# Loads of the next k, v and q held back until all four transposing DMAs of a batch have landed, with the work from the third batch on ordered anew

## The chip, the cores and the metric

The kernel runs on one core of a Trainium2 chip. Its time is the device time of one execution in microseconds (us), lower is better, and the comparison is between the kernel before and the kernel after one change. The core has four engines that compute, each with its own stream of instructions: TensorE (PE, with PEld for its weight loads), VectorE (DVE), ScalarE (ACT) and GpSimd (POOL). SyncE (SP) does nothing here but issue DMAs. An engine works its stream in order, and an instruction may wait for semaphores that other engines or landed DMAs have raised.

## The reference, cut to what matters

A linear attention over 8 batches of 8 heads, 576 rows and 64 columns a head, with an RMS norm, is followed by a residual MLP of width 512. The MLP first mixes the 576 rows (tokens) and then the columns (channels, 512 to 2048 and back).

```python
kv  = np.einsum('bhsd,bhse->bhde', k, v)
out = np.einsum('bhsd,bhde->bhse', q, kv)
rms = np.sqrt(np.mean(out * out, axis=-1, keepdims=True) + 1e-06)
x   = out / rms * g_norm          # heads side by side: (8, 576, 512)
a1  = alpha1 * x + beta1
u   = x + lam * np.einsum('ts,bsd->btd', w_tok, a1)
a2  = alpha2 * u + beta2
res = u + lam * (np.maximum(a2 @ w_ch1, 0.0) @ w_ch2)
```

## The kernel before

**Batches.** The 8 batches are numbered 0 to 7. The 576 rows of one are held as four blocks of 128 rows and a tail of 64; the tails of an even batch and of the odd one behind it share one tile of 128 rows (`xt`, transposed `a2l`). `xm` has four places for the blocks of batches, `a2m` two for their transposes.

**Stages of a batch.** `kv` (L639, L645) multiplies k by v in f32. `norm` makes a block of the attention's output: PE products from `kvc` and the transposed q (L730, f32), then square, sum, root and scaling on ACT and DVE (L697 to L715, the last step L715 writing x), and on POOL the token mixer's operand `rm` (L718). `tok` is the token mixing (PE L813) with its residual add on DVE (L823, which writes `xm`). `a2_dma` turns a finished block round so that the channel MLP can contract over channels: POOL casts it to bf16 (`a2b`, L901), then a DMA of SP's queue transposes it into `a2m` (L914). `ch1` (PE L1091) multiplies `a2m` by the first weights, ACT applies the relu into `hh` or `ht` (L920). The second product goes by a scheme of fewer, wider combinations of blocks (`strassen`, PE L1213 with 256 columns; sums of blocks on DVE, L1175; kept products are copied by ACT, L1243, and added into `xm` by POOL, L1246; the last addends come from DVE, L1251). For batches 0 and 1 it is plain (`ch2`, L1152), and for batches 6 and 7 ch1 runs for both together (`pair`). `store` sends a finished block out by SP's queue (L1343, L1348, L1265).

**What is woven.** While the MLP of batch b runs, `attention(b + 2)` and `mix(b + 2)` are written behind it, and the order below weaves them into its products, so that PE always has some product to do.

**The loads.** `attention(b)` issues the loads of batch b + 1, which go into the buffers that batch b has just been read from: k and v by POOL's queue, each as 512 rows (1 MB, L1467, `kr` and `vr`) and 64 tail rows (L1471), and q by SP's queue in four pieces with 32-column rows (L1459, `qs`). All are tied to a transposing DMA of the batch before through the list `landing`:

```python
load_kv(b + 1, landing.get(b - 1, ()))                              # L1524
load_q(b + 1, landing.get(b - 1, [P.lastw[("w2", 3)][0]]))          # L1525
```

`landing[b]` is set by `a2_dma`, which is called for c = 0 to 3 (the blocks) and, in odd batches, for c = 4 (the shared tails):

```python
if c < 3:                                                           # L916
    landing[b] = [o]                                                # L917
```

Each call overwrites the entry, so that the loads of batch b + 2 wait for the transposing DMA of block 2 of batch b, and for no other. The DMAs of block c signal one semaphore a c: d_50 to d_53 for blocks 0 to 3, d_54 for the tails; d_38 is that of v's tail rows.

**The order.** Nothing is scheduled on the chip or by a compiler. Every operation gets a number as it is written, and a table `ORDER` lists the numbers in the order in which they are put into the engines' streams (`op:bank` names the PSUM bank of a product, `a+b` weaves two groups of products). A second table, `GATES`, adds waits: `i: j` makes operation i wait for j. `Prog.replay` reads both, and `synchronize` turns what depends on another engine or on a DMA into semaphores. Numbers that matter below: 448, 452, 456 and 460 are batch 2's four casts (L901), 650 to 657 steps of `weight_sums`, which prepares weight sums on DVE; 586 to 589, 747 to 750, 940 to 943 and 1093 to 1096 are q loads, each gated on the tail rows of the same batch's k or v.

Of the kernel before, what the change touches and what calls it, by code (L numbers as in the profile page):

```python
# [103 lines left out]
"""  # L104

GATES = {23: 52, 38: 67, 39: 73, 40: 163, 124: 151, 125: 213, 204: 196, 233: 269, 234: 216, 235:
# [8 lines left out]


class Op:


    __slots__ = ("tile", "q", "kind", "cost", "lat", "fns", "idx", "deps", "raw", "alloc", "tiles", "at",  # L120
                 "pos", "waits", "inc", "clock", "slot", "nbytes", "ns", "val", "form", "bias")

    def __init__(self, q, kind, cost, lat, fns, pri, idx):
# [236 lines left out]
def bass_transnormer_attn__then__resmlp_affine_kernel(  # L360
# [15 lines left out]
    with ExitStack() as stack:  # L376
# [515 lines left out]
        def a2_dma(b, c, t=None):  # L892
# [20 lines left out]
            o = P.dma(  # L913
                "SP", "t%d" % c, 0.7, lambda e: e.dma_start_transpose(dst, a2b[:, c]),  # L914
                r=[("a2b", c)], w=dk, issue=0.6)
            if c < 3:  # L916
                landing[b] = [o]  # L917

        def relu(dst, t, keys, f=None):
            P.op("ACT", act(512, 0 if f is None else 1), lambda e: e.activation(  # L920
# [704 lines left out]
```

## Time and profile before

| | |
|---|---|
| Runs, us | 334.7, 330.46, 332.15 (median 332.15) |
| Profiled execution, us | 332.92 |
| Its span, from the first to the last instruction, us | 331.1 |
| Mean granted clock of TensorE | 0.990 |
| DMA | 48.15 MB in 108,532 packets, 145 GB/s mean |

The profile is of one execution of the kernel. Its page gives the busy time and share of each engine, the span in 40 equal slices (of 8.28 us here; a digit is the busy share in tenths, PEclk the clock that TensorE was granted), the DMA queues, the chain of work that ended last (each step followed back to what released it), and the costliest groups of instructions, as line, engine, operation and tiles with count, busy time and mean. Other views are asked for: waits by what released them, a timeline of a stretch, the busy times in a list of stretches, and of DMAs the time from issue to landing. SPq is SP's queue: its rows are the issue of DMAs, not their transfer. A wait for several semaphores shows as one for the last of them.

The costliest single groups of PE's instructions are L1091 (ch1, 96.8 us), L1213 (strassen, its largest group 43.9), L730 (norm, 43.2), L1152 (ch2, 36.8), L639 (kv, 34.7) and L813 (token mixing, 29.3).

### The profile page before, as it was taken

Reading aid. Unit: us, or ns where it says so; the run is one execution under the profiler, and the core shown is the slowest. Engines: PE = TensorE matmul, PEld = TensorE weight load, DVE = VectorE, ACT = ScalarE, POOL = GpSimd, SP = SyncE. Lnnn points to the kernel's source line nnn. Section 1 sums busy time; section 2 is a strip of 40 time slices with the busy share of each in tenths; the row PEclk is TensorE's granted clock in tenths of the full one; section 3 lists DMA queues with packets and bytes.
Section 4 is the critical chain, followed back from the end, with each engine's and each line's share of the span. In section 5 each row is a group of like instructions: output and inputs, shape, how many; then the busy total and the mean of one; then the engine's idle time right before and its main releaser. Section 6 shows DMA issues by size and latency. Waiting matters only on the chain.

```text
span 331.1 us, 6149 instructions
## 1 busy us (share of the span) xinstructions
PE 322.1 (97%) x2411; PEld 220.3 (67%) x2441; DVE 251.3 (76%) x460; ACT 176.8 (53%) x362; POOL 140.1 (42%) x146
## 2 busy tenths in 40 slices
PE   8999999999999999969999999999999999999996
PEld 8777664555766455847558975587658554579985
DVE  3595178776999998706986389898899889997673
ACT  5674772249444473614872566742785057865440
POOL 3699036998063353610625241727135600012320
PEclk9999999999999999969999999999999999999999
DMA  7999998999912991995825992796050150000125
GB/s 259 319 259 258 215 247 196 198 143 259 272 40 48 263 207 25 159 226 124 206 33 122 231 177 61 133 305 104 34 157 3 40 166 4 0 2 0 50 88 183
DMA packets 108532, 48.15 MB, mean 145 GB/s; under 512 B 82061, under 2 KB 101717, under 8 KB 108504
## 3 DMA queue, kind: packets, MB, share of 16 engines
q1 hardware_dynamic: 72160, 25.00, 33.1%
q0 software_dynamic: 26800, 21.38, 32.9%
q10 hardware_dynamic: 9544, 1.39, 2.5%
q8 instruction: 19, 0.31, 0.4%
q14 instruction: 9, 0.07, 0.1%
HBM read 38.82 MB, written 9.44 MB: 146 GB/s over the span
## 4 chain that ended last, share of the span: by engine, by line
PE 88%; DVE 4%; DMA 3%; ACT 2%; SPq 1%; POOL 1%; issue 1%
PE ps L1091 24%; PE ps L1213 22%; PE ps L1152 9%; PE ps L813 9%; PE ps L1032 7%; PE ps L730 3%; DMA a2m<-a2b 3%; PE ps L639 2%; PE ps L1105 2%; PE ps L973 2%; PE ps L466 1%; SPq L914 1%; PE ps L595 1%; PE ps L858 1%; DVE small L781 1%; PE ps L617 1%
## 5 line engine op out<-in xcount | busy, mean ns | idle before, releaser
L1091 PE MATMUL ps<-a2m,w 128*128 128x512 bf16 x369 | 96.8, 386 | 0.4 <-issue 0.2
L718 POOL TENSOR_TENSOR rm<-xm,la_bc 128x512 bf16<-128x512 f32 x28 | 35.4, 1272 | 68.4 <-DVE xm L715 50.0
L1091 PEld LDWEIGHTS ps<-a2m,w 128*128 128x128 bf16 x384 | 36.4, 98 | 40.8 <-DMA a2m<-a2b 3.4
L920 ACT ACTIVATE hh<-ps,b 128x512 bf16<-128x512 f32 x72 | 47.2, 686 | 12.4 <-PE ps L1091 7.8
L1246 POOL TENSOR_TENSOR xm<-xm,tmp 128x512 f32<-128x512 f32 x18 | 22.7, 1268 | 60.0 <-ACT sq L983 28.2
L730 PE MATMUL ps<-kvc,qt 128*128 128x128 f32 (+1 forms) x140 | 43.2, 409 | 3.3 <-DMA a2m<-a2b 3.3
L1213 PE MATMUL ps<-w,hh 128*128 128x256 bf16 x344 | 43.9, 279 | 0.0
L1213 PEld LDWEIGHTS ps<-w,hh 128*128 128x128 bf16 x344 | 34.1, 100 | 7.1 <-issue 0.7
L1152 PE MATMUL ps<-w,hh 128*128 128x512 bf16 x137 | 36.8, 385 | 0.1
L639 PE MATMUL ps<-vr,kr 128*128 128x128 f32 x112 | 34.7, 408 | 0.0
L1251 DVE TENSOR_TENSOR xm<-ps,xm 128x512 f32<-128x512 f32 x24 | 16.3, 686 | 21.9 <-PE ps L1213 14.8
L700 DVE TENSOR_REDUCE small<-sq 128x8 f32<-128x512 f32 (+1 forms) x35 | 23.3, 678 | 10.3 <-ACT sq L697 10.1
L813 PE MATMUL ps<-rm,wt 128*128 128x512 bf16 x108 | 29.3, 382 | 0.3 <-issue 0.2
L730 PEld LDWEIGHTS ps<-kvc,qt 128*128 128x128 f32 (+1 forms) x140 | 27.6, 198 | 2.1 <-ACT qt L1480 0.4
L901 POOL CAST a2b<-xm 128x512 bf16<-128x512 f32 x24 | 14.2, 611 | 32.6 <-DVE xm L823 18.5
L697 ACT ACTIVATE sq<-ps 128x512 f32<-128x512 f32 (+1 forms) x35 | 20.5, 594 | 13.2 <-PE ps L730 12.9
L708 DVE TENSOR_TENSOR ps<-ps,small 128x512 f32<-128x512 f32 (+1 forms) x35 | 24.3, 696 | 0.8
L920 ACT ACTIVATE hh<-ps 128x512 bf16<-128x512 f32 x32 | 17.5, 597 | 11.9 <-PE ps L1091 11.8
L639 PEld LDWEIGHTS ps<-vr,kr 128*128 128x128 f32 x112 | 22.4, 200 | 1.6
L1243 ACT ACTIVATE tmp<-ps 128x512 f32<-128x512 f32 (+1 forms) x20 | 11.5, 575 | 20.6 <-PE ps L1213 20.6
L1152 PEld LDWEIGHTS ps<-w,hh 128*128 128x128 bf16 x144 | 13.4, 97 | 13.4 <-issue 0.4
L1480 ACT ACTIVATE qt<-qp 128x576 fp32r<-128x576 f32 x24 | 15.9, 679 | 11.1 <-DVE qp L1477 11.0
(216 smaller groups left out, 618.2 us busy)
## 6 DMA issues: line engine op xcount, KB each, us to landing
out_dram<-xm SPq DMA_DIRECT2D x32, 256.0 KB, 2.4
kr<-in_k_dram POOLq DMA_DIRECT2D x7, 1024.0 KB, 6.7
vr<-in_v_dram POOLq DMA_DIRECT2D x7, 1024.0 KB, 8.2
qs<-in_q_dram SPq DMA_DIRECT2D x20, 288.0 KB, 5.0
w<-in_moe_w_ch_dram POOLq DMA_DIRECT2D x8, 512.0 KB, 10.5
xm<-in_q_dram SPq DMA_DIRECT2D x8, 288.0 KB, 5.1
qs<-in_v_dram SPq DMA_DIRECT2D x4, 288.0 KB, 5.4
w<-in_k_dram SPq DMA_DIRECT2D x4, 288.0 KB, 5.4
```

The source lines that it names most:

```text
L639: P.mm("fill", 128, [lambda e, t=t, c=c, h=h, o=128 * (h % 4): e.matmul(t.ap()[:, o:o + 128], kr4[:, h, c:c + 2, :].rearrange("p c d -> p ...
L700: P.op("DVE", dve(n), lambda e: e.tensor_reduce(out=st, in_=sq[rs, s3, 0:nst, :], axis=AX.X, op=ALU.add), r=[("sq", s3)], w=[("sm", s4)])
L708: P.op("DVE", dve(n), lambda e: e.tensor_tensor(out=grp(ps()), in0=grp(ps()), in1=st[..., None].to_broadcast([rs.stop - rs.start, nst, DH] ...
L718: P.op("POOL", pool(n), lambda e: e.tensor_tensor(out=r, in0=x.rearrange("p h e -> p (h e)"), in1=la, op=ALU.mult), r=xks + ["la"], w=rks)
L730: P.mm("fill", 128, [lambda e, p=p: e.matmul(dst(p), qt[:, p, cs], kvc[:, i, p, :], start=(p == 0), stop=(p == 3)) for p in range(4)], r=[ ...
L813: P.mm("fill", 512, [lambda e, sc=sc: e.matmul(t.ap(), wt[:, sc if sc < 4 else tw(b), 128 * c:128 * c + 128], rsrc(b, sc, al), start=(sc = ...
L920: P.op("ACT", act(512, 0 if f is None else 1), lambda e: e.activation(dst, t.ap(), ACT.Relu, bias=0.0 if f is None else b1[:, f:f + 1]), r ...
L1032: P.mm("main", 512, [lambda e, i=i: e.matmul(t.ap(), lhs[:, i, 128 * x + o:128 * x + o + 128], rhs[:, i, :], start=(first and i == 0), sto ...
L1091: P.mm("main", 512, [lambda e, dj=dj: e.matmul(t.ap(), w1[:, dj, 128 * fj:128 * fj + 128], a2m[:, b % 2, dj, :], start=(dj == 0), stop=(dj ...
L1152: P.mm("main", 512, [lambda e, fj=fj, t=t, c=c: e.matmul(t.ap(), (ht[:, fj, 128 * c:128 * c + 128] if c < 4 else hl[:, fj, :]), w2[:, fj, ...
L1213: P.mm("main", 256, [lambda e, c=c, fj=fj: e.matmul(t.ap()[:, 256 * c:256 * c + 256], at[:, fj, 128 * c:128 * c + 128], rhs(fj), start=(fi ...
L1246: P.op("POOL", pool(256 * n), lambda e, cs=cs, f=f: e.tensor_tensor(out=X[:, cs, f], in0=X[:, cs, f], in1=two(tmp[:, s]), op=ALU.add), r=x ...
```

## The change

`landing[b]` becomes, for batches 3 and up, the list of the transposing DMAs of all four blocks. The loads of batches 5, 6 and 7 so wait for all four of batches 3, 4 and 5. For batches up to 2 the entry stays that of block 2 alone, and the tails (c = 4) are in no list. The tables are written anew: `ORDER` from about 95 us of the program on (in the streams, from row 258 of PE's), and `GATES` in part. No operation is added or removed; each engine has as many instructions as before.

```diff
 GATES = {23: 52, 38: 67, 39: 73, 40: 163, 124: 151, 125: 213, 204: 196, 233: 269, 234: 216, 235:
-    260, 237: 298, 371: 465, 379: 650, 399: 275, 448: 654, 452: 654, 466: 465, 468: 650, 586:
-    585, 587: 585, 588: 585, 589: 585, 597: 651, 621: 651, 632: 652, 636: 652, 640: 652, 644:
+    260, 237: 298, 371: 465, 379: 650, 399: 275, 448: 654, 452: 655, 456: 655, 460: 655, 466:
+    465, 468: 467, 586: 585, 587: 585, 588: 585, 589: 585, 597: 533, 605: 656, 613: 656, 632:
...
-406:4+498:1 414:5+534:7 468 379 495 407 408 422:2+535 415 416 430:0+536 502:3 469 423 499 431 503
...
             o = P.dma(
                 "SP", "t%d" % c, 0.7, lambda e: e.dma_start_transpose(dst, a2b[:, c]),
                 r=[("a2b", c)], w=dk, issue=0.6)
-            if c < 3:
-                landing[b] = [o]
+            if c < 4:
+                landing[b] = landing.get(b, []) + [o] if b > 2 else [o] if c < 3 else landing[b]
```

What the streams look like at the places that matter is shown below: the line, the operation with its tiles (written, then read) and the shape, the semaphores that it waits for in brackets, and x for equal ones in a row.

**The loads of batch 5 on POOL.** The four loads stand behind the cast of the shared tails of batches 2 and 3. Before:

```order
L901 CAST a2b<-xt 128x512 [waits s_DVE]
L1471 DMA vr<-in_v_dram 64x8x64 [waits d_52]
L1471 DMA kr<-in_k_dram 64x8x64
L1467 DMA vr<-in_v_dram 128x8x256
L1467 DMA kr<-in_k_dram 128x8x256
L1246 TENSOR_TENSOR xm<-xm,tmp 128x2x256 [waits s_ACT,s_DVE]
L1246 TENSOR_TENSOR xm<-xm,tmp 128x2x256 [waits s_ACT] x2
```

and after:

```order
L901 CAST a2b<-xt 128x512 [waits s_DVE]
L1471 DMA vr<-in_v_dram 64x8x64 [waits d_52,d_50,d_51,d_53]
L1467 DMA vr<-in_v_dram 128x8x256
L1467 DMA kr<-in_k_dram 128x8x256
L1246 TENSOR_TENSOR xm<-xm,tmp 128x2x256 [waits s_DVE,s_ACT]
L1246 TENSOR_TENSOR xm<-xm,tmp 128x2x256 [waits s_ACT]
L1246 TENSOR_TENSOR xm<-xm,tmp 128x2x256
L1471 DMA kr<-in_k_dram 64x8x64
```

The first load waits for four transposes where it waited for one, and the load of k's tail rows moved behind the three adds.

**The adds of batch 2's token mixing on DVE**, with the last step of a norm (L715) and the sums of weights for batch 1's last products and batch 2's first (L1175, L1133) among them. Before:

```order
L823 TENSOR_TENSOR xm<-ps,xm 128x512 [waits s_PE] x3
L715 TENSOR_TENSOR xt<-ps,g_bc 64x512
L823 TENSOR_TENSOR xm<-ps,xm 128x512 [waits s_PE]
L700 TENSOR_REDUCE small<-sq 128x8 [waits s_ACT]
L1175 TENSOR_TENSOR ws<-w,ab_bc 128x1024
L1133 TENSOR_SCALAR w<-w,ab 128x2048 [waits s_PE]
L1133 TENSOR_SCALAR w<-w,ab 128x2048 [waits s_DVE]
```

and after:

```order
L823 TENSOR_TENSOR xm<-ps,xm 128x512 [waits s_PE]
L1175 TENSOR_TENSOR ab_bc<-w 128x1024
L823 TENSOR_TENSOR xm<-ps,xm 128x512 [waits s_PE]
L715 TENSOR_TENSOR xt<-ps,g_bc 64x512
L823 TENSOR_TENSOR xm<-ps,xm 128x512 [waits s_PE]
L1175 TENSOR_TENSOR ws<-w,ab_bc 128x1024 [waits s_DVE]
L823 TENSOR_TENSOR xm<-ps,xm 128x512 [waits s_PE]
L700 TENSOR_REDUCE small<-sq 128x8 [waits s_ACT]
```

The adds, which the casts L901 of batch 2 wait for, now have three other operations between them, where they had one.

**The transposes of batch 2 and the q loads of batch 4 on SP.** Before:

```order
L914 DMA_TRANSPOSE a2m<-a2b 128x4x128 [waits s_POOL] x3
L914 DMA_TRANSPOSE a2m<-a2b 128x4x128
L1343 DMA out_dram<-xm 128x512
L1459 DMA qs<-in_q_dram 32x72x32 [waits d_38]
L1459 DMA qs<-in_q_dram 32x72x32 x3
```

and after:

```order
L914 DMA_TRANSPOSE a2m<-a2b 128x4x128 [waits s_POOL]
L1343 DMA out_dram<-xm 128x512 x2
L914 DMA_TRANSPOSE a2m<-a2b 128x4x128 [waits s_POOL] x3
L1459 DMA qs<-in_q_dram 32x72x32 [waits d_38]
L1459 DMA qs<-in_q_dram 32x72x32 x3
L1348 DMA out_dram<-xt 64x512 [waits s_DVE]
```

Two stores of finished blocks now stand between the first transpose and the other three.

133 rows, old and new, of tables (GATES, ORDER) are left out of this document.

## The prediction

> **What bounds the kernel now.** The page first: busy shares, the slices, the chain that ended last.
>
> ```profile
> PE 322.1 (97%) x2411; PEld 220.3 (67%) x2441; DVE 251.3 (76%) x460; ACT 176.8 (53%) x362; POOL 140.1 (42%) x146
> PE   8999999999999999969999999999999999999996
> PEclk9999999999999999969999999999999999999999
> PE 88%; DVE 4%; DMA 3%; ACT 2%; SPq 1%; POOL 1%; issue 1%
> ```
>
> PE is busy 97% of 331.1 us, and the two rows by slices show one hole, in slice 18 (about 141 to 149 us), where PE and its granted clock both fall to 6 tenths. The waits of PE, longest first, and the stretches around that hole (us; busy time of PE, PEld, DVE, ACT, POOL; granted clock; DMA share; GB/s) come next.
>
> ```profile
> PE ps L730 <- DMA a2m<-a2b: 3.3, 1, 3.3
> PE ps L466 <- DVE fil L465: 1.0, 1, 1.0
> PE ps L813 <- issue: 0.2, 1, 0.2
> ...
> 135.00:141.40 6.40, 6.40 (x60) 5.62 (x58) 3.78 (x6) 2.94 (x5) 5.07 (x6) 1.00 1.44 190
> 141.40:144.70 3.30, 0.07 (x2) 0.02 (x2) 0.69 (x1) 0.00 (x0) 0.50 (x1) 0.83 1.71 300
> 144.70:150.50 5.80, 5.77 (x24) 3.79 (x26) 0.09 (x1) 1.18 (x2) 0.00 (x0) 0.51 0.80 141
> ```
>
> PE stood 3.3 us for a transposing DMA, and then worked 5.8 us at a clock of 0.51. No other wait of PE after the first microseconds is above 0.2 us. So whatever a new order does, it can win little beyond this hole, and it can lose anywhere. The timeline of the queues (start us, duration) tells which transfers met there.
>
> ```profile
> 130.53 3.02 SPq L914 DMA_TRANSPOSE a2m<-a2b  x2
> ...
> 133.64 0.74 POOL L1471 DMA_DIRECT2D vr<-in_v_dram  x1 [1.54 <-DMA a2m<-a2b]
> ...
> 134.23 2.61 SPq L914 DMA_TRANSPOSE a2m<-a2b  x2
> ...
> 135.03 0.93 POOL L1467 DMA_DIRECT2D vr<-in_v_dram  x1
> ...
> 135.93 0.92 POOL L1467 DMA_DIRECT2D kr<-in_k_dram  x1
> ```
>
> The queue of SP issued batch 3's block transposes 2, 0 (130.53) and 1, 3 (134.23, so the last about 135.6). POOL waited for number 2 alone and put batch 5's loads between them. Landing times (min/median/max) of single transposes: all 28 with their median, then the last one of batch 3, of batch 2 (issued 106.56) and of batch 5 (212.16).
>
> ```profile
> DMA to landing us min/median/max: 2.4/2.5/9.1
> DMA to landing us min/median/max: 9.1/9.1/9.1
> DMA to landing us min/median/max: 4.9/4.9/4.9
> DMA to landing us min/median/max: 5.7/5.7/5.7
> ```
>
> 2.5 us is the common case; the three slow ones all had the 1 MB loads in flight. 135.6 + 9.1 = 144.7 is the moment PE starts again.
>
> **The change, part by part.**
>
> 1. *Four waits instead of one, batch 3.* The loads of batch 5 now start when all four transposes have landed, so number 3 meets none of them. At 2.5 us it lands at 135.6 + 2.5 = 138.1, which is 3.3 us before PE runs dry at 141.4. Gain: the 3.3 us, whole. What hides the transpose from then on is the batch 2 products that stand ahead of ch1(3); were they shorter by 3.3 us, the wait would be back.
>
> 2. *The clock after it.* From 144.7 to 150.5 PE did 5.8 x 0.51 = 2.96 us of full-speed work; without the hole 2.84 us fall away too. Row first: the clock fell inside a hole of 3.3 us (0.83 on average, so for about a third of it). The Trainium skill, "TensorE: Matmul & The Clock Gate", section "What's actually happening", says the clock halves after at least one idle window of about 3.4 us, and that the windows run free of the kernel. By that figure alone a 3.3 us hole would cost no clock, and the sum would be 332.9 - 3.3 + 0.8 = 330.4; the measured clock decides. Gain of 1 and 2: 6.1 us.
>
> 3. *Batch 4 and its loads of batch 6.* The last transpose of batch 4 was issued at 174.95 and lands 2.5 us later, at 177.45; the first load of batch 6 starts behind that:
>
> ```profile
> 174.95 1.27 SPq L914 DMA_TRANSPOSE a2m<-a2b  x1
> ...
> 177.78 0.95 POOL L1467 DMA_DIRECT2D kr<-in_k_dram  x1
> ```
>
> So the added wait is 0 here.
>
> 4. *Batch 5 and its loads of batch 7.* The first of them was issued at 211.0, and it now starts when the last transpose lands. That one was issued at 212.16, so 212.16 + 2.5 = 214.7, or 3.7 us later. The lower end is the 1.5 us that POOL stood ahead of batch 3's loads, if the new order issues all four transposes as closely. The two 1 MB loads were issued last but one and last, at 212.4 and 213.3; landings of POOL's loads there stand between the first issue and the first product that reads them:
>
> ```profile
> 210.99 0.74 POOL L1471 DMA_DIRECT2D vr<-in_v_dram  x1
> ...
> DMA to landing us min/median/max: 7.7/9.3/10.9
> ...
> 229.37 0.30 PE L639 MATMUL ps<-vr,kr 128*128 128x128 f32 x1
> ```
>
> The later one landed at 213.3 + 10.9 = 224.2, and its first product starts at 229.37: 5.2 us of cover against 1.5 to 3.7. Cost 0. The q loads queue on SP behind them (the gates tie them to v's tail rows), 12.6 us of issue from 214.15, and are read by the DVE transposes at 232.24. They landed about 2.4 us ahead (229.9 = last issue 225.5 + 4.4). What is moved is the start; the bytes are the same, and the loads no longer share with transposes: 0 to 1.3 us, taken 0.
>
> ```profile
> 214.15 12.59 SPq L1459 DMA_DIRECT2D qs<-in_q_dram  x4
> DMA to landing us min/median/max: 4.4/9.2/12.2
> 232.24 0.77 DVE L1477 STREAM_TRANSPOSE qp<-qs 128x576 f32<-128x576 f32 x1
> ```
>
> 5. *What queues behind POOL's wait.* Now the three adds of batch 2's kept products (L1246) stand behind a wait to about 138.1 and three issues of 0.7 to 0.9 us: up to 2.5 us later than the 138.17 of this row.
>
> ```profile
> 138.17 3.72 POOL L1246 TENSOR_TENSOR xm<-xm,tmp 128x512 f32<-128x512 f32 x3 [1.33 <-DVE hh L1175]
> ```
>
> DVE's last adds (L1251) need them, and PE's next products need the banks these free. The new order puts the transpose's landing nearer to its cast, and a norm with a product and ch1(3)'s first tile (1.7 + 0.9 us of PE) between the last product and the first that needs the bank. Ends 0 and 1.3 us, taken 0.
>
> 6. *The third batch (batch 2) keeps the wait for transpose 2 alone, and its order is new.* Before and now:
>
> ```profile
> 100.73 2.00 DVE L823 TENSOR_TENSOR xm<-ps,xm 128x512 f32<-128x512 f32 x3
> 102.64 0.67 DVE L715 TENSOR_TENSOR xt<-ps,g_bc 64x512 f32<-64x512 f32 x1
> 104.62 0.71 DVE L1175 TENSOR_TENSOR ws<-w,ab_bc 128x1024 bf16<-128x1024 bf16 x1
> ...
> 102.06 1.72 POOL L901 CAST a2b<-xm 128x512 bf16<-128x512 f32 x3 [4.43 <-DVE xm L823]
> 106.71 0.95 POOL L1467 DMA_DIRECT2D kr<-in_k_dram  x1 [1.93 <-DMA a2m<-a2b]
> ...
> 102.70 5.13 SPq L914 DMA_TRANSPOSE a2m<-a2b  x4
> ...
> 108.61 2.98 PE L1152 MATMUL ps<-w,hh 128*128 128x512 bf16 x12
> 111.58 1.67 PE L1091 MATMUL ps<-a2m,w 128*128 128x512 bf16 x7
> ```
>
> Transpose 0 was issued last (106.56) and landed 4.9 us later at 111.5, when PE wanted it at 111.58: no slack at all. In the new order the cast for transpose 2 comes behind L715 and L1175 on DVE: 102.73 + 0.67 + 0.71 = 104.1, cast 0.6, issue 104.8, where it was 103.94. That is 0.86 us later. Two transposes follow it as before, so the last meets the kr load at the same distance (0.15 us) and lands at 111.5 + 0.86 = 112.35. Cost 0.8 us of PE wait; ends 0 (if the last landed in 2.5 us) and 5.0 us (if it took 9.1: 107.4 + 9.1 = 116.5 against 111.5). I take 0.8, because the geometry is that of the row with 4.9. So short a hole is below the 2.3 us that passed before the clock fell in the measured one, so no clock is lost.
>
> 7. *The rest of the order.* The counts of products are the same. Twelve of L730's products now stand among 256-column products (three norms woven with L1213). A weight load of f32 takes 0.19 to 0.20 us and a 256-column product 0.11 (x48 in 5.24), so the ends are 0 and 12 x 0.09 = 1.1 us. Where one followed such a product, the next product started 0.15 us after it, not later than in the steady pattern (0.29 a pair). I take 0.
>
> ```profile
> 172.48 5.24 PE ps L1213 x48
> 151.92 0.19 PEld L730 LDWEIGHTS ps<-kvc,qt 128*128 128x128 f32 x1
> 151.95 0.30 PE L730 MATMUL ps<-kvc,qt 128*128 128x128 f32 x1
> 152.10 0.39 PE L1091 MATMUL ps<-a2m,w 128*128 128x512 bf16 x1
> ```
>
> Sum: -3.3 - 2.8 + 0.8 = -5.3. The profiled execution took 332.92 us (span 331.1 and 1.8 around it), so 327.6. It lies 0.8 above the median of the runs, 332.15, from which the same sum gives 326.9. I say 327.4, 1.4% under the median.
>
> **The rivals.**
>
> *A. The third batch's last transpose is hit in full.* Batch 3's number 3 had v's 1 MB load 0.55 us ahead of it and took 9.1; batch 2's last had kr's 0.15 behind it and took 4.9. If two stores now ahead of transpose 2 on SP move the last one behind the load, PE waits 116.5 - 111.5 = 5.0 us and about 2.9 us go with the clock: 332.9 - 6.1 + 7.9 = 334.7, above before. It decides from a landing of about 7.5 us on, where wait and clock together pass 6.1. For it: no slack, and this batch alone got no added wait. Against: the distance between the two issues follows from one wait and does not change.
>
> *B. The waits come back elsewhere.* Points 4, 5 and 7 each at the upper end (1.3, 1.3, 1.1 us), in part: 329 to 331.
>
> *C. The loads are not what slows the transpose.* If load and transposes merely took turns, a transpose would at most double, from 2.5 to 5.0 us. The 4.9 and nearly the 5.7 fit that, and the 9.1 does not. Then part of the 9.1 comes from SP's own queue, where a store (at 133.6, between the two pairs of transposes) stands ahead, and the new order has stores there too. The wait is back in full if nothing of the 9.1 goes: 333 us, no change; a wait of any size needs more than 141.4 - 135.6 = 5.8 us. For it: that number. Against: the median of all 28 is 2.5, though stores stand on SP's queue around many of them. The Trainium skill, "DMA: Bandwidth & Descriptors", section "Queues, rings and completion order", has a DMA engine go round between the queues it has work for, a whole packet each; that is the taking of turns, told as a rule, and of the three slow landings the trace agrees on two.
>
> *D. More than 2%.* The hole and its clock are all that PE can win: 332.9 - 6.1 = 326.8 is the floor, and 2% under the median is 325.5. It needs runs of before with a longer hole than the profiled one (the slowest of three took 334.7).
>
> **How the numbers follow.** Forecast 0.62 (326.0 to 328.8), A 0.09, B 0.14, C 0.06, D 0.09. The likeliest is 327.4. The range 325.6 to 331.0 holds the forecast and B and leaves out A, C and most of D, together about 0.2. Two per cent of 332.15 is 6.6 us, about what a measurement of this kernel can tell from no change: faster by more 0.13, within 0.83, slower by more (over 338.8, A and B together) 0.04. So I expect a real gain of some 5 us that stays inside that bound.
>
> **What would show it.** Batch 3's four transposes land in 2.4 to 3 us; PE has no wait for one there; the clock reads 1.0 in the slices around 145 us. Near 112 us PE waits about 0.8 us for batch 2's last transpose, with a landing near 5. The first POOL load of batch 5 waits for the transposes, and L1246 behind it is not on the chain. I am wrong if a second hole above 2 us shows in the row of PE, if the clock falls anywhere past 60 us, or if batch 3's last transpose still takes over 5 us.

## The result, and the profile after

| | before | after |
|---|---|---|
| Median of the runs, us | 332.13 (330.31 to 334.7, 6 runs) | 327.12 (326.38 to 328.19, 6 runs) |
| Profiled execution, us | 332.92 | 327.01 |
| Its span, us | 331.1 | 325.2 |
| Mean granted clock of it | 0.990 | 1.000 |

The ratio is 0.985, with a 95% interval of 0.980 to 0.990: faster by 1.5%, a gain that is clear of noise and inside the 2% that the chances went by. The forecast was 327.4. Here and below, ratios leave out executions more than 1.5% above the fastest of the same kernel, while counts of executions by their clock take all of them.

The busy shares, the slices and the chain of the page of the changed kernel:

```profile
PE 320.0 (98%) x2441; PEld 218.7 (67%) x2441; DVE 252.1 (78%) x460; ACT 176.7 (54%) x362; POOL 141.7 (44%) x146
PE   7999999999999999999999999999999999999996
PEclk9999999999999999999999999999999999999999
PE 92%; DVE 3%; ACT 2%; DMA 2%; SPq 0%; issue 0%
```

The 6 in slice 18 is gone from both rows, and PE's share of the chain rose from 88% to 92%. PE's longest waits, and the stretches around the old hole (columns as before):

```profile
PE ps L466 <- DVE fil L465: 1.1, 1, 1.1
PE ps L617 <- DMA w<-in_k_dram: 0.7, 1, 0.7
...
136.00:142.80 6.80, 6.80 (x66) 6.10 (x65) 3.77 (x7) 2.56 (x6) 5.47 (x6) 1.00 0.96 210
142.80:150.00 7.20, 7.20 (x57) 5.39 (x54) 5.14 (x10) 4.10 (x9) 1.43 (x2) 1.00 1.34 237
```

Both waits stand in the first 8 us, where the loads of batch 0 arrive; behind them PE waits for no transpose. The timeline of batch 3's last transposes and batch 5's loads, and the landing of all four transposes (minimum, median, maximum):

```profile
129.17 2.53 SPq L914 DMA_TRANSPOSE a2m<-a2b  x2
...
132.37 2.12 SPq L914 DMA_TRANSPOSE a2m<-a2b  x1
...
136.01 0.73 POOL L1471 DMA_DIRECT2D vr<-in_v_dram  x1 [2.56 <-DMA a2m<-a2b]
136.74 0.91 POOL L1467 DMA_DIRECT2D vr<-in_v_dram  x1
...
139.84 3.73 POOL L1246 TENSOR_TENSOR xm<-xm,tmp 128x512 f32<-128x512 f32 x3 [1.31 <-ACT tmp L1243]
...
DMA to landing us min/median/max: 2.4/2.9/4.2
...
142.77 1.03 PE L1091 MATMUL ps<-a2m,w 128*128 128x512 bf16 x4
```

The last transpose is issued at 132.4 and takes 3.3 us, so it lands at 135.7; POOL stood 2.56 us for it, and PE reads it at 142.8. The 4.2 is the transpose issued at 130.42: no 1 MB load was in flight, so a transpose can take that long without one. Two things changed at once: the loads wait longer, and the transposes are issued some 3 us earlier (the last at 132.4 instead of 135.6) while PE needs them 1.4 us later. Which of the two removed the hole can't be read from this profile; the experiments tell it.

### The profile page after: what moved, and what is told of

It is laid out like the page before. It is cut to its first block, busy times and chain, and to the rows that moved or that the text cites. A ratio compares the mean times of both kernels' runs of the same rounds, so it can differ in the third digit from the quotient of the medians.

```text
span 325.2 us, 6190 instructions
## 1 busy us (share of the span) xinstructions
PE 320.0 (98%) x2441; PEld 218.7 (67%) x2441; DVE 252.1 (78%) x460; ACT 176.7 (54%) x362; POOL 141.7 (44%) x146
## 4 chain that ended last, share of the span: by engine, by line
PE 92%; DVE 3%; ACT 2%; DMA 2%; SPq 0%; issue 0%
PE ps L1091 26%; PE ps L1213 25%; PE ps L1152 10%; PE ps L813 9%; PE ps L1032 7%; PE ps L730 3%; PE ps L1105 2%; PE ps L639 2%; PE ps L973 2%; DMA w<-in_k_dram 2%; PE ps L858 1%; DVE small L781 1%; PE ps L617 1%; PE ps L595 1%; PE ps L878 1%; DVE xm L787 1%
## 5 line engine op out<-in xcount | busy, mean ns | idle before, releaser
L1091 PE MATMUL ps<-a2m,w 128*128 128x512 bf16 x384 | 98.2, 384 | 0.0
L1246 POOL TENSOR_TENSOR xm<-xm,tmp 128x512 f32<-128x512 f32 x18 | 23.1, 1300 | 54.8 <-ACT tmp L1243 49.6
L1213 PE MATMUL ps<-w,hh 128*128 128x256 bf16 x344 | 42.7, 273 | 0.0
L730 PE MATMUL ps<-kvc,qt 128*128 128x128 f32 (+1 forms) x140 | 42.6, 396 | 0.0
L1152 PE MATMUL ps<-w,hh 128*128 128x512 bf16 x144 | 38.2, 385 | 0.0
L1213 PEld LDWEIGHTS ps<-w,hh 128*128 128x128 bf16 x344 | 32.4, 98 | 6.3 <-issue 0.8
L901 POOL CAST a2b<-xm 128x512 bf16<-128x512 f32 x24 | 14.8, 628 | 35.3 <-DVE xm L823 24.2
L813 PE MATMUL ps<-rm,wt 128*128 128x512 bf16 x112 | 30.0, 381 | 0.0
L730 PEld LDWEIGHTS ps<-kvc,qt 128*128 128x128 f32 (+1 forms) x140 | 27.1, 194 | 2.7 <-issue 0.8
L1152 PEld LDWEIGHTS ps<-w,hh 128*128 128x128 bf16 x144 | 13.4, 97 | 13.2 <-issue 0.4
```

The lines of the kernel that those rows point to most:

```text
L730: P.mm("fill", 128, [lambda e, p=p: e.matmul(dst(p), qt[:, p, cs], kvc[:, i, p, :], start=(p == 0), stop=(p == 3)) for p in range(4)], r=[ ...
L813: P.mm("fill", 512, [lambda e, sc=sc: e.matmul(t.ap(), wt[:, sc if sc < 4 else tw(b), 128 * c:128 * c + 128], rsrc(b, sc, al), start=(sc = ...
L1091: P.mm("main", 512, [lambda e, dj=dj: e.matmul(t.ap(), w1[:, dj, 128 * fj:128 * fj + 128], a2m[:, b % 2, dj, :], start=(dj == 0), stop=(dj ...
L1152: P.mm("main", 512, [lambda e, fj=fj, t=t, c=c: e.matmul(t.ap(), (ht[:, fj, 128 * c:128 * c + 128] if c < 4 else hl[:, fj, :]), w2[:, fj, ...
L1213: P.mm("main", 256, [lambda e, c=c, fj=fj: e.matmul(t.ap()[:, 256 * c:256 * c + 256], at[:, fj, 128 * c:128 * c + 128], rhs(fj), start=(fi ...
L1246: P.op("POOL", pool(256 * n), lambda e, cs=cs, f=f: e.tensor_tensor(out=X[:, cs, f], in0=X[:, cs, f], in1=two(tmp[:, s]), op=ALU.add), r=x ...
```

## The experiments

Every run stands beside runs of the kernel before on the same chip. The first two, with the kernels before and after, make a square of old and new order by old and new wait.

**The new order with the old wait.** The two lines in `a2_dma` go back to what they were.

```diff
-            if c < 4:
-                landing[b] = landing.get(b, []) + [o] if b > 2 else [o] if c < 3 else landing[b]
+            if c < 3:
+                landing[b] = [o]
```

> The new order with the wait of before: the loads of batches 5, 6 and 7 wait for block 2's transpose alone. Theory M (what slows a transpose is a 1 MB load whose issue ended ahead of its own; who brings that about, a wait or an order, does not matter): batch 3's four transposes are issued by 134.3 us in the new order, and the loads stand behind a cast that ends at 133.5, so the first 1 MB load is issued by about 135, behind the last transpose. That one lands in under 4 us, PE has no hole, 327.1 us as with the change, within 1 us. Rival W (the added waits bring the gain): transpose 3 of batch 3 takes 6 to 9 us again and lands at 139 to 142 us; PE needs it at 142.8, so part of the hole or nothing shows, with more on DVE and ACT behind; 328 to 333 us. Rival O (the new order alone brings the gain by other means): 327 us too; it is told from M by the run of the old order with the new waits.

Measured: 327.25 us (326.71 to 328.19), ratio 0.987 (0.983 to 0.992). That is the changed kernel's time without the added waits, so rival W falls. The last transpose of batch 3 in the timeline, v's 1 MB load, and the landing of that transpose:

```profile
133.07 1.22 SPq L914 DMA_TRANSPOSE a2m<-a2b  x1
...
133.82 0.90 POOL L1467 DMA_DIRECT2D vr<-in_v_dram  x1
...
DMA to landing us min/median/max: 3.6/3.6/3.6
```

The transpose's issue ends at 134.29 and the load's at 134.72, 0.43 us behind it. Both are in flight together for some 2 us, and yet the transpose takes 3.6 us, not 9.

**The old order with the new waits.** The change's two lines in the kernel before; two loads of tail rows of batch 7 had to go behind two transposes in `ORDER`, which moves nothing within POOL's or SP's stream.

```diff
-            if c < 3:
-                landing[b] = [o]
+            if c < 4:
+                landing[b] = landing.get(b, []) + [o] if b > 2 else [o] if c < 3 else landing[b]
```

> The order of before with the added waits alone (on PE, DVE and ACT nothing moves, on POOL only the waits; on SP nothing). Theory M: transpose 3 of batch 3 lands about 2.5 us behind its issue, at some 138.1 us on the time scale of before, the loads of batch 5 start there, the hole of 3.3 us and its 2.8 us at half clock go, and 326 to 328.5 us are left; the adds L1246 behind the waiting load come up to 4.5 us later, and what they cost on PE is the upper end. Rival O (the order is what gains, the waits do nothing): 332 us, and the hole stays. Rival B (the wait moves the loss to POOL's adds): no wait for a transpose on PE, but one of 2 to 4 us for L1251 or for a bank behind it; 329 to 332 us.

Measured: 329.8 us (328.97 to 331.51), ratio 0.996 (0.993 to 0.999): 1.6 us of the 5. Rival B came about, with a smaller wait than its 2 to 4 us, and M's 326 to 328.5 was too low. The transposes of batch 3, the wait of PE, and POOL's stream behind its own wait:

```profile
DMA to landing us min/median/max: 2.5/2.5/2.6
...
PE ps L1213 <- DVE xm L1251: 1.5, 1, 1.5
...
138.80 0.74 POOL L1471 DMA_DIRECT2D vr<-in_v_dram  x1 [6.02 <-DMA a2m<-a2b]
...
141.99 3.75 POOL L1246 TENSOR_TENSOR xm<-xm,tmp 128x512 f32<-128x512 f32 x3
```

All four transposes land in 2.5 us, so the hole at them is gone although the order is the old one, which speaks for M against rival O. But POOL stands 6 us in front of the loads, and the adds behind them start at 141.99 instead of 138.17 (PE's products run 0.7 us later in this execution before that, so some 3.1 us of it are the wait's). PE waits 1.5 us for the DVE add that needs them.

**The old order, with a wait for two transposes.** Batch 5's loads wait for blocks 2 and 0.

```diff
-                landing[b] = [o]
+                landing[b] = (landing[b] if c else []) + [o] if b == 3 and c != 1 else landing[b] if b == 3 else [o]
```

> The order of before; the loads of batch 5 wait for the transposes of blocks 2 and 0 (which lands at 134.6 us), not for 1 and 3. Theory M: the loads start 1.4 us later, so the first 1 MB load's issue ends at about 137.1, 0.5 us behind that of transpose 3 (136.6), which then lands in 2.5 to 4 us though the loads are in flight for most of that; no hole, 326 to 328.5 us. Rival S (load and transpose share the DMA engines as long as both are in flight): transpose 3 takes 5 to 8 us, so it lands at 140.5 to 143.5; a hole of 0 to 2 us, 328 to 331 us.

Measured: 327.29 us (326.37 to 328.04), ratio 0.987 (0.982 to 0.992). One more awaited transpose in the old order brings as much as the whole change. Transposes 1 and 3 of batch 3, and v's 1 MB load, with the landing of number 3:

```profile
135.34 2.60 SPq L914 DMA_TRANSPOSE a2m<-a2b  x2
...
137.61 0.91 POOL L1467 DMA_DIRECT2D vr<-in_v_dram  x1
...
DMA to landing us min/median/max: 3.7/3.7/3.7
```

The load's issue ends at 138.52, the transpose's at 137.94. Again 0.6 us in the right direction is enough, although SP's store still stands between the transposes. That removes rival C of the prediction as the cause of the 9.1 us, and rival S with its 5 to 8 us. In this execution PE waited 0.9 us near 112 us (the wait is put down to a DVE add; batch 2's last transpose had taken 5.7 us).

**The kernel before again**, unchanged, for the clock of each execution.

> The kernel before itself, to see the clock and the span of each of its executions. If the hole at 141 us always costs clock as in the profiled execution (mean clock 0.99), all executions show 0.99 and 330 to 335 us. If the clock falls only in some of them, those with 1.00 stand some 2.8 us below those with 0.99, which would explain the spread of 330.3 to 334.7 us.

Measured: 331.75 us. With the runs of before that stood beside the other experiments, 85 executions fall into three groups by their mean clock: 23 at 0.999 or 1.00 (median 329.8 us), 48 at 0.994 or 0.995 (332.2) and 13 at 0.989 or 0.99 (333.9); one lies between, at 0.993. So the clock falls in some executions only, and those at 0.99 stand 4.1 us above those at 1.00, not 2.8. The profile of this run is one of the first group; the stretches at its hole and behind it are

```profile
141.10:144.20 3.10, 0.19 (x3) 0.04 (x1) 0.69 (x1) 0.00 (x0) 0.62 (x1) 1.00 1.48 292
144.20:150.00 5.80, 5.61 (x47) 4.69 (x48) 1.55 (x3) 1.18 (x2) 0.00 (x0) 1.00 1.00 197
```

with the same hole of 3.1 us and a clock of 1.00. The execution that the prediction was worked out on, at 0.990, is of the smallest of the three groups.

**The old order with batch 2's loads held back too.** As with the two transposes, and batch 4's loads wait for blocks 2 and 3.

```diff
-            if c < 3:
-                landing[b] = [o]
+            if c in {2: (2, 3), 3: (0, 2)}.get(b, (2,)):
+                landing[b] = landing.get(b, []) + [o]
```

> The order of before; the loads of batch 5 wait for the transposes of blocks 2 and 0, as in the run before, and the loads of batch 4 for those of blocks 2 and 3 (landing at 107.5 and later), where before they waited for block 2. Theory M: the 1 MB load of batch 4 now ends its issue about 1 us behind that of batch 2's last transpose, which lands in 2.5 us where it took 4.2 to 5.7; the PE wait of up to 1.1 us at 112 us goes, and 326.3 to 327.0 us are left, 0.3 to 1 below the 327.29 of the run before and level with or below the kernel with the change. The load lands by about 120.2, still ahead of its first product at 120.9. Rival N (that landing costs nothing on the whole): 327.3 us again. Rival K (the later loads make the first product of batch 4 wait): 328 us, with a wait for a load at 121 us.

Measured: 327.22 us (326.64 to 328.41), ratio 0.982 (0.979 to 0.986) to a kernel before that took 332.44 in this batch of runs. Batch 2's last transposes landed in 2.5 us and the wait near 112 us is gone from the profile, but the time is that of the run without this: rival N, and not the 326.3 to 327.0 of M. Whatever the late landing cost, it is below what these runs resolve. No version beats the changed kernel: 327.1 to 327.3 us is what four of the kernels without the hole take.

**Big loads first.** POOL issues batch 5's two 1 MB loads ahead of its tail rows; old order and wait.

```diff
-682:0 681 641 633 643 737 644 735 647 731 738 558 637 645 736 683 648 741 694:5 686:3 746 744 745
-743 688:7 733 687 685 734 739 698:2 695 689 696 740 699 732 692 693 705 706 701 700 702 703 709:1
+682:0 681 641 633 643 737 644 735 647 731 738 558 637 645 736 683 648 741 694:5 686:3 745 743 746
+744 688:7 733 687 685 734 739 698:2 695 689 696 740 699 732 692 693 705 706 701 700 702 703 709:1
```

> The order and the wait of before, but POOL issues the two 1 MB loads of batch 5 ahead of its two loads of tail rows, so 1.4 us earlier. Theory M (the lead of the 1 MB loads over a transpose counts): the first 1 MB load now ends its issue at 134.3 us, ahead of the transposes of block 1 (135.3) and of block 3 (136.6); both are slow, 6 to 10 us, the last lands at 144 to 147, the hole is 3 to 6 us, and more of the executions lose clock: 332 to 337 us. Rival T (the small loads of tail rows, many short packets, are what slows transposes): with these behind the big ones, transpose 3 lands earlier, in 5 us or less, the hole goes, 327 to 329 us.

Measured: 331.68 us (330.11 to 333.85), ratio 0.997 (0.993 to 1.000). The hole is there (3.5 us) though the tail rows now stand behind the 1 MB loads, so rival T falls; but M's time was too high. The transpose of block 1 now has the load 0.92 us ahead of it (load's issue end 134.92, its own 135.84), and it took 8.3 us, where in the kernel before it took 3.8:

```profile
133.97 0.95 POOL L1467 DMA_DIRECT2D vr<-in_v_dram  x1 [1.69 <-DMA a2m<-a2b]
...
134.54 3.26 SPq L914 DMA_TRANSPOSE a2m<-a2b  x2
...
DMA to landing us min/median/max: 8.3/8.3/8.3
```

The first of the two issues took 1.30 us. The last transpose took 9.2 us, as before, though both loads were ahead of it, v's by 2.9 us. So the delay does not go on growing with the lead.

**Holes of three lengths.** In the changed kernel a product of batch 2 waits for v's 1 MB load of batch 5.

```diff
-GATES = {23: 52, 38: 67, 39: 73, 40: 163, 124: 151, 125: 213, 204: 196, 233: 269, 234: 216, 235:
+GATES = {713: 745, 23: 52, 38: 67, 39: 73, 40: 163, 124: 151, 125: 213, 204: 196, 233: 269, 234: 216, 235:
```

> The changed kernel with one wait put in: the product of batch 2 that starts at about 139.8 us waits for v's 1 MB load of batch 5 (landing at 142.5), a hole of about 2.7 us on PE. Theory G (the clock falls only behind a hole of at least about 3 us, and in some executions only): all executions at a clock of 1.00, 327.1 + 2.7 = 329.8 us. Rival H (any hole over 2.3 us costs clock, as the prediction read it from one execution): a clock of 0.995 or less, 331 to 333 us.

The longer one has `705: 745`, the shorter one `714: 745`.

> As the run with the hole of 2.7 us, but the product that starts at 137.2 us waits for the same load: a hole of about 5.3 us. Theory G: every execution loses clock, one or two steps of about 1.6 us, 327.1 + 5.3 + 1.6 to 3.2 = 334.0 to 335.6 us, clock 0.99 to 0.995. Rival H2 (the loss grows with the hole without steps): one clock value near 0.985 in all, 336 to 338 us.

> The changed kernel with one wait put in: the product that starts at about 140.7 us, one later than in the run with the hole of 3.2 us, waits for v's 1 MB load of batch 5: a hole of 2.0 to 2.6 us. If the clock can fall behind a hole of this size, some of the executions show 0.995 and stand 1.5 us above the others, which lie at 329.3 to 329.7 us; if not, all show 1.00 and 329.3 to 329.7 us.

| Hole in the profile, us | Median, us | Executions at a clock of 1.00 / 0.995 / 0.99 |
|---|---|---|
| 1.8 | 330.1 | 7 / 3 / 0 |
| 3.2 | 332.06 | 3 / 4 / 2, and one at 0.98 |
| 6.0 | 334.87 | 0 / 1 / 9 |

The wait of PE in the first row's profile, an execution at 1.00:

```profile
PE ps L1213 <- DMA vr<-in_v_dram: 1.8, 1, 1.8
```

All three holes came out a little different from plan (2.0 to 2.6, 2.7 and 5.3). H falls with the second row: 3 of 10 lost nothing. With the third row H2 falls: all ten lose clock, nine of them two steps, at 334.87 us, as G said. G's lower bound of 3 us is in doubt by the first row: 3 of 10 executions lost clock. It isn't refuted, since only one execution's hole is on record, and a run below without a made hole (the old order with the adds between the loads) has 1 of 12 executions at 0.995, where the profile of another one shows a hole of 0.5 us. A mean clock doesn't tell where it fell. The steps are real, as these rows of the runs with 3.2 and 6.0 us show:

```profile
140.40:143.60 3.20, 0.07 (x1) 0.00 (x1) 0.00 (x0) 0.89 (x2) 3.20 (x3) 0.91 1.49 381
143.60:146.40 2.80, 2.77 (x14) 1.94 (x15) 0.00 (x0) 0.00 (x0) 1.08 (x2) 0.50 1.69 321
```

```profile
137.00:143.10 6.10, 0.15 (x2) 0.00 (x1) 2.19 (x5) 0.00 (x0) 1.19 (x2) 0.86 1.22 264
143.10:148.30 5.20, 5.17 (x25) 3.61 (x26) 0.00 (x0) 1.17 (x2) 0.88 (x1) 0.51 0.99 176
```

The time at half clock is twice the missing share of each stretch: 2 x 0.09 x 3.2 + 2.8 = 3.4 us in the first, 2 x 0.14 x 6.1 + 5.1 = 6.8 in the second, and in the profile of before 2 x 0.17 x 3.3 + 2 x 0.49 x 5.8 = 6.8. One or two pieces in some 330 us are also what a mean clock of 0.995 or 0.99 stands for. In these three profiles it comes in pieces of 3.4 us, one or two. How much of a piece falls into the hole, where it costs nothing, differs.

**The old order with the adds between the loads.** As the old order with the new waits, but the two loads of tail rows stand behind the adds.

```diff
-682:0 681 641 633 643 737 644 735 647 731 738 558 637 645 736 683 648 741 694:5 686:3 746 744 745
-743 688:7 733 687 685 734 739 698:2 695 689 696 740 699 732 692 693 705 706 701 700 702 703 709:1
-707 742 697 708 704 710 713 711 714 712 751:4+807:0 716 715 717 721 718 722 750 719 723
+682:0 681 641 633 643 737 644 735 647 731 738 558 637 645 736 683 648 741 694:5 686:3 745 743 688:7 733 687 685 734 739 698:2 695 689 696 740 699 732 692 693 705 706 701 700 702 703 709:1
+707 742 697 708 704 710 713 711 714 712 746
+744 751:4+807:0 716 715 717 721 718 722 750 719 723
```

> The order of before with the added waits, and of batch 5's four loads on POOL only the two of 1 MB ahead of the three adds L1246; the two loads of tail rows stand behind the adds. Theory Q (what the added wait costs in the old order is the adds that queue behind the waiting loads): the adds come 1.4 us earlier than with all four loads ahead (at 140.6 instead of 142.0), the PE wait of 1.5 us for L1251 at 146.5 us shrinks to 0 to 0.3, and 328.0 to 328.5 us are left, against 329.8. Rival Q2 (the cost lies elsewhere, the wait at L1251 only stands in front of another): 329.5 us or more, with a new wait of PE in place of that one.

Measured: 328.54 us (327.44 to 330.54), ratio 0.994 (0.991 to 0.997): 1.3 us of the cost are back, at the edge of what Q said. PE's wait and the adds in the profile (that of the fastest execution):

```profile
PE ps L1213 <- DVE xm L1251: 0.5, 1, 0.5
...
139.84 3.73 POOL L1246 TENSOR_TENSOR xm<-xm,tmp 128x512 f32<-128x512 f32 x3
```

So the queue behind POOL's wait was about half of the cost. The other 1.3 us to the new order stay unexplained: the one profile is of the fastest execution, 1.1 us below the median.

## Why the prediction was right, and where it was not

The time, the sign and the mechanism came out: one transpose behind 1 MB loads made the hole, and with it gone PE runs through. Of the signs that were named, the clock, the wait of the loads and L1246, which is not on the chain, came as said; the landing of batch 3's transposes (2.4 to 4.2 us instead of 2.4 to 3) and PE's wait near 112 us (none instead of 0.8) did not. By its own steps:

**Step 1, the hole of 3.3 us.** It went, whole. But the step gave the gain to the four waits, and that attribution failed. In the new order they aren't needed (327.25 without them), and in the old one they bring 1.6 us. The order brought the gain by itself: the transposes go out earlier, and the loads stand behind the cast of the tails anyway, so that the 1 MB load's issue ends behind the last transpose's. The landing at 138.1, too, was worked out on the old order's issue times; it was 135.7. The square of the four kernels, in us:

| | old wait | new waits |
|---|---|---|
| old order | 331.41 (beside 327.25 and 329.8) | 329.8 |
| new order | 327.25 | 327.12 (beside a before of 332.13) |

**Step 2, the clock, 2.8 us.** Right by the rows of the profiled execution, too large for the median. Against the group of before that lost no clock (329.8), the other two stand 2.4 and 4.1 us higher, differences in the hole included, and the median execution lies in the middle one. (The 2.3 us that step 6 takes to have passed in the hole before the clock fell come out of the same rows as 2.2: 3.3 less 2 x 0.17 x 3.3.) By the page's figure of the Trainium skill that the step weighed, no clock should have been lost at 3.3 us, but its mean was 0.83 inside the hole of the profile of before and 0.91 inside the made one of 3.2 us, and 62 of the 85 executions lost some. With that threshold the trace doesn't agree. It does agree with the length of the window that "TensorE: Matmul & The Clock Gate" of the Trainium skill, section "What's actually happening", states (some 3.4 us), in pieces of 3.4 us; that some executions lose a piece and others none fits windows that run free of the kernel, as the section says, but was not tested.

**Steps 3 and 4, the loads of batches 6 and 7.** Cost 0, as said. POOL stood for the transposes before both, also before batch 6's, where step 3 had taken no added wait, and no product waited:

```profile
172.85 0.94 POOL L1467 DMA_DIRECT2D kr<-in_k_dram  x1 [1.18 <-DMA a2m<-a2b]
...
207.62 0.94 POOL L1467 DMA_DIRECT2D vr<-in_v_dram  x1 [1.17 <-DMA a2m<-a2b]
...
DMA to landing us min/median/max: 6.8/8.1/9.4
...
224.49 0.31 PE L639 MATMUL ps<-vr,kr 128*128 128x128 f32 x1
```

It stood 1.2 us in both places, under the 1.5 to 3.7 of step 4; in the new order with the old wait it stood for no transpose there. With the loads' last issue at about 209.9, 9.4 us put the landing at 219.3, 5.2 us ahead of the product: as much cover as before.

**Step 5, what queues behind POOL's wait.** The mechanism was named, and in the old order it costs 1.5 us, more than the upper end of 1.3. In the new order it costs 0, since the transposes land earlier against PE's work. So the 0 that was taken is right only together with the new order.

**Step 6, batch 2's last transpose, +0.8 us.** This term was mis-sized: it was 0. PE's first product of batch 2 starts without a wait. The transpose did come late, by 1.4 us (105.38 instead of 103.94) where 0.86 was worked out, but "the same distance" was wrong:

```profile
105.38 3.84 SPq L914 DMA_TRANSPOSE a2m<-a2b  x3
...
108.24 1.37 POOL L1467 DMA_DIRECT2D kr<-in_k_dram  x1 [1.77 <-DMA a2m<-a2b]
...
DMA to landing us min/median/max: 2.5/2.5/2.6
```

The load's issue took 1.37 us instead of 0.95 and ended at 109.61, 0.39 us behind the last transpose (109.22); before, it had ended 0.17 ahead of it (107.66 against 107.83). All four landed in 2.5 us. What seems to decide is the end of the load's issue against the end of the transpose's; the step compared the starts (the last section weighs the two).

**Step 7, the rest of the order.** Cost 0, as taken. A product of L730 with two of L1213 behind it starts every 0.30 us:

```profile
141.50 0.31 PE L730 MATMUL ps<-kvc,qt 128*128 128x128 f32 x1
141.65 0.39 PE L1213 MATMUL ps<-w,hh 128*128 128x256 bf16 x2
141.80 0.30 PE L730 MATMUL ps<-kvc,qt 128*128 128x128 f32 x1
```

**The sum.** Forecast -3.3 - 2.8 + 0.8 = -5.3. The measured -5.0 is 329.8 - 327.1 = 2.7 for the hole and 332.1 - 329.8 = 2.3 for the clock in the middle group. Two terms too large by some half a microsecond each and one that wasn't there made a sum that is nearly right; the closeness of the total is partly luck.

**The rivals.** A didn't happen: in the new order batch 2's last transpose landed in 2.5 us. The place was well chosen, since in the old order it takes up to 5.7 us, and PE waited 0.9 us there in one profile. B came about in the old order only. C is ruled out as the cause of the 9.1 us: stores stand between the transposes in the runs where they land in 2.5 to 4.2 us. D didn't happen; its chance of 0.09 and the 0.13 given to the same outcome didn't fit each other.

## What to carry to other kernels

When a short transfer on one queue is needed soon and a large load waits on another, let the short one's issue end first: here half a microsecond decided between some 4 and 5 to 6 us, and 1.3 us between 4 and 9. Hold the load back by the least that does it; a longer wait in an in-order stream makes everything behind it late, and here PE waited 1.5 us for that until the order made room. And before costing a clock loss from one profile, look at the clock of all executions: the profiled one can be the rare case.

## What the runs showed of the hardware that was not expected

How long a transposing DMA took against the lead of the 1 MB load, which is the end of the transpose's issue minus the end of the load's (positive: the load was first):

| Lead, us | Kernel, transpose | Issue to landing, us |
|---|---|---|
| -0.58, -0.56 | old order, two transposes, and with batch 2 held back too; batch 3 | 3.7, 4.0 |
| -0.44 to -0.42 | before and before again (block 1), and new order, old wait; batch 3 | 3.6 to 3.9 |
| -0.39 to -0.36 | after, and the four other profiles of the new order, batch 2 | 2.5 or 2.6 |
| 0.13 to 0.15 | old order, five profiles, batch 5 | 5.2 to 6.4 |
| 0.16, 0.17 | old order, six profiles, batch 2 | 4.2 to 5.7 |
| 0.87, 0.88 | before again, before, batch 3, block 3 | 9.2, 9.1 |
| 0.92 | big loads first, batch 3, block 1 | 8.3 |
| 2.9 | big loads first, batch 3, block 3 | 9.2 |

With a negative lead a transpose took 2.5 to 4.0 us, which is no more than the transposes of blocks took with no 1 MB load in flight (2.4 to 4.2 us). By the starts of the issues the rows stand in nearly the same order, but there the slow row of batch 5 (-0.23 to -0.21) and the fast one of batch 2 (-0.29 to -0.26) would be parted by 0.03 us; by the ends it is half a microsecond and the sign. So the ends are the likelier measure, and no run was made to tell the two apart.

With the load 0.9 us ahead, the transpose landed nearly together with v's load: at 144.6 and 144.9 in the profile of before, at 142.8 and 143.0 with the big loads first, where the load was issued 0.57 us earlier. If the two queues took turns, packet by packet, as "DMA: Bandwidth & Descriptors" of the Trainium skill, section "Queues, rings and completion order", states, a transpose would be slowed and not held until the load is through; these rows don't look like turns. The others are not so clear: with a lead of 0.13 to 0.17 us the transpose landed 1.4 to 4.1 us before the load, and the last row's, with v's and k's loads both ahead, landed at 145.1, between them (143.0 and 147.5). What in the DMA engines makes it so was not tried.
